# Another order of the same operations in a hand-planned attention and feed-forward kernel

The kernel runs on one core of one Trainium2 chip. The metric is the time of one execution on the device, in microseconds (us); lower is better. All runs named here gave correct results.

Names: PE is the tensor engine, PEld its weight loads, DVE is VectorE, ACT is ScalarE, POOL is GpSimd, SP is SyncE. An engine's name with a q behind it (SPq, POOLq) is its sequencer, which issues transfers.

## The reference

```python
# q, k, v: 8 batches x 8 heads x 576 rows x 64; w_phi: 64 x 128
def phi(x):
    proj = einsum('bhsd,df->bhsf', x, w_phi)
    proj = proj - max(abs(proj), axis=-1, keepdims=True)
    return concatenate([exp(proj), exp(-proj)], axis=-1)
q_p, k_p = phi(q), phi(k)
kv  = einsum('bhsf,bhsd->bhfd', k_p, v)
z   = sum(k_p, axis=2)
num = einsum('bhsf,bhfd->bhsd', q_p, kv)
den = einsum('bhsf,bhf->bhs', q_p, z)[..., None] + 1e-06
x   = (num / den) with heads joined            # 4608 tokens x 512
out = (maximum(x @ w_gate, 0) * (x @ w_val)) @ w_out    # 512 -> 1536 -> 512
```

Linear attention comes first, then a gated feed-forward layer on its output. The feed-forward matmuls are four fifths of PE's work. They can begin only when the first rows of `x` are there, so the kernel has a *head* (load, project, k'v, divide, transpose, with PE often waiting), a *middle* (feed-forward of one batch woven with the attention of later batches) and a *tail* (last copy, last stores).

## The kernel before

The kernel writes down every operation once, with what it depends on and which buffers and PSUM banks it needs. It then replays them in the order of a text table. An entry `34P00` is operation 34, on PE, with slots 0 and 0 for the buffers that it opens; the letters are P (PE), A (ACT), D (DVE), G (POOL) and S (SP). `w29` is 29 warm-up matmuls on a tile of zeros, `z3` are three of them in the next operation's own bank. The table is one global list, but each engine sees only its own entries, in that order.

```python
def read(self, table):
    order, last_load, last_turn, zeros = [], None, None, 0
    for entry in table.split():
        if entry[0] == "w":
            order += [(self.warm(), PE)] * int(entry[1:])
            continue
        ...
        n, letter, slots = re.fullmatch(r"(\d+)([A-Z])(\w*)", entry).groups()
        o, e = self.ops[int(n)], LETTERS[letter]
        new = [b for b in (*o.banks, *o.bufs) if b.slot is None]
        for b, slot in zip(new, slots, strict=True):
            b.slot = int(slot, 36)
        ...
        order.append((o, e))

# k_item: projection of k in two 64-row halves, then exp on ACT, maxima on DVE
for i in range(4):
    for x in range(2):
        half = slice(D * x, D * (x + 1))             # 64 rows
        nc.tensor.matmul(pair[x].t[:, F * i : F * (i + 1)],
                         lhsT=kT.t[half, 4 * u + i, :], rhs=w2[half, x, :])    # L390
...
# the scaling of V by the exponentials of the maxima, on POOL for the most part
eng.tensor_tensor(vs.t[:, :, :, 0:D], vn..., e()..., op=ALU.mult)              # L416
eng.tensor_copy(vs.t[:, :, :, D], e())                                         # L423

# q_cols: the same for q, again in 64-row halves
nc.tensor.matmul(pair[x].t, lhsT=w2[half, x, :], rhs=cols(half))               # L507

# k_kv (L483) and q_num (L601): 128-row matmuls of 65 columns
# q_num's end: xu = u * r on POOL (L629), then a transpose and a copy to xT
# ffn: four matmuls of 512 columns a group (L670 up, L708 down)

# the stores of the last group of rows: each tile of 128 rows goes to two batches
for x, e in enumerate((SP, ACT) if t == 3 else (SP, SP)):
    def store_part(x=x, e=e, t=t, place=place, lo=lo, hi=hi):
        r0 = S * (2 * t + x) + SF
        engines[e].dma_start(out=out[r0 : r0 + SM, lo:hi],
                             in_=place()[SM * x : SM * (x + 1), lo:hi])        # L735
    op(e, 0.5, store_part, [c_], [ob], ...)
```

## Time and profile before

| | the kernel before |
|---|---|
| time, median of the first three runs | 379.24 us (378.41 to 379.54) |
| profiled span | 377.3 us |
| first feed-forward matmul starts at | 31.4 us |
| warm-up matmuls | 146 |
| waits of PE (start to start, beyond the usual spacing) | 17.8 us |
| end of the last matmul to end of the span (*) | 4.8 us |

(*) Here and below a matmul is counted as done one spacing (0.22 us for 512 columns) after its start. The trace's modelled end of the last matmul lies 0.16 us later; the 4.6 us of the prediction are counted from there.

The rows of the page that carry the argument are quoted in the prediction. The difference between 379.24 and 377.3 is time outside the profiled instructions. This profile was taken in a run of 379.24 us.

### The profile page before, as it was taken

How to read it: one execution, taken by the hardware profiler on the slowest of the kernel's cores; microseconds unless marked ns; L12 is line 12 of the kernel's file. 1: busy time of each engine (PE TensorE's matmuls, PEld its weight loads, DVE VectorE, ACT ScalarE, POOL GpSimd, SP SyncE). 2: the span in 40 equal slices, each digit the busy share in tenths (PEclk: the TensorE clock that was granted, in tenths of full speed). 3: DMA queues.
4: the chain of work that ended last, by engine and by line, in shares of the span. 5: the costliest groups of instructions: out<-in, count | busy, mean ns of one | idle time of the engine just before them, and what ended most of it. 6: DMA issues, size and time to landing. Idle time of an engine off the chain costs nothing.

```text
span 377.3 us, 8560 instructions
## 1 busy us (share of the span) xinstructions
PE 365.1 (97%) x3259; PEld 206.3 (55%) x3305; DVE 264.4 (70%) x642; ACT 232.8 (62%) x532; POOL 172.0 (46%) x206
## 2 busy tenths in 40 slices
PE   8889999999999999999999999999999999999995
PEld 7677797445656555464455544654465544444452
DVE  5989998777897977868965887679748645234121
ACT  5989975699599557756894569669853121222211
POOL 8698773459594335592693237713641300000000
PEclk9999999999999999999999999999999999999999
DMA  8999976798967593899667244951200500011016
GB/s 152 245 214 238 198 107 105 136 267 149 153 137 112 110 228 85 144 153 181 136 141 159 84 86 114 166 120 30 70 2 15 127 2 27 14 48 65 0 57 167
DMA packets 83288, 44.73 MB, mean 119 GB/s; under 512 B 54064, under 2 KB 76464, under 8 KB 83248
## 3 DMA queue, kind: packets, MB, share of 16 engines
q0 software_dynamic: 32656, 23.27, 36.4%
q1 hardware_dynamic: 50352, 20.75, 24.8%
q8 instruction: 26, 0.43, 0.5%
q10 hardware_dynamic: 240, 0.16, 0.2%
q14 instruction: 14, 0.11, 0.1%
HBM read 37.81 MB, written 9.44 MB: 125 GB/s over the span
## 4 chain that ended last, share of the span: by engine, by line
PE 88%; POOL 4%; ACT 3%; DVE 2%; issue 1%; DMA 1%; SPq 0%; POOLq 0%; DVEq 0%
PE ps L670 49%; PE ps L708 24%; PE ps L601 5%; PE ps L483 4%; PE ps L507 2%; PE ps L390 2%; ACT kp L351 2%; POOL vs L416 1%; DMA w<-in_w_phi_dram 1%; DVE mq L517 1%; POOL xu L629 1%; PE ps L642 1%; PE ps L532 0%; POOL wg_sb L297 0%; PE ps L437 0%
## 5 line engine op out<-in xcount | busy, mean ns | idle before, releaser
L676 ACT CAST val<-ps 128x512 bf16<-128x512 f32 (+1 forms) x120 | 64.9, 569 | 76.6 <-PE ps L670 68.1
L679 DVE SCALAR_TENSOR_TENSOR h<-ps,val 128x512 bf16<-128x512 f32 (+1 forms) x120 | 73.4, 626 | 43.9 <-PE ps L670 28.1
L708 PE MATMUL ps<-wo_sb,h 128*128 128x512 bf16 (+1 forms) x422 | 100.4, 373 | 1.1
L670 PE MATMUL ps<-xT,wg_sb 128*128 128x512 bf16 (+1 forms) x418 | 95.7, 354 | 0.7
L670 PE MATMUL ps<-xT,wv_sb 128*128 128x512 bf16 (+1 forms) x423 | 95.7, 355 | 0.5
L351 ACT ACTIVATE qp<-ps 128x512 bf16<-128x512 f32 x144 | 80.4, 643 | 11.4 <-PE ps L507 10.2
L629 POOL TENSOR_TENSOR xu<-u,r 128x512 bf16<-128x512 f32 x36 | 37.3, 1042 | 105.7 <-DVE r L626 58.2
L351 ACT ACTIVATE kp<-ps 128x512 bf16<-128x512 f32 x128 | 71.4, 631 | 9.7 <-PE ps L390 8.1
L416 POOL TENSOR_TENSOR vs<-vn,ek 128x1024 bf16<-128x1024 f32 x31 | 59.1, 1906 | 23.2 <-ACT ek L364 14.9
L670 PEld LDWEIGHTS <-wv_sb 128*128 128x128 bf16 x480 | 44.0, 98 | 40.4 <-issue 1.9
L670 PEld LDWEIGHTS <-wg_sb 128*128 128x128 bf16 x480 | 44.5, 98 | 39.4 <-issue 0.7
L708 PEld LDWEIGHTS <-h 128*128 128x128 bf16 x444 | 41.1, 98 | 44.8 <-issue 1.6
L401 DVE TENSOR_REDUCE mk<-ps 128x4 f32<-128x512 f32 x64 | 41.4, 676 | 2.9 <-PE ps L390 1.5
L517 DVE TRANSPOSE_TENSOR_REDUCE mq<-ps 128x16 f32<-128x512 f32 x56 | 37.5, 695 | 6.1 <-PE ps L507 3.1
L616 DVE TENSOR_TENSOR u<-ps,t 128x195 f32<-128x195 f32 (+3 forms) x120 | 37.2, 329 | 2.0
L601 PEld LDWEIGHTS <-qp 128*128 128x128 bf16 x640 | 30.4, 98 | 14.2 <-issue 0.2
L609 DVE TENSOR_TENSOR t<-ps,cq 128x195 f32<-128x195 f32 (+1 forms) x84 | 26.2, 329 | 15.1 <-PE ps L601 12.6
L601 PE MATMUL ps<-kv,qp 128*128 128x65 bf16 x640 | 33.7, 193 | 0.1
L483 PEld LDWEIGHTS <-kp 128*128 128x128 bf16 x512 | 21.7, 98 | 6.0 <-issue 2.1
L483 PE MATMUL ps<-vs,kp 128*128 128x65 bf16 x512 | 23.1, 193 | 1.9 <-POOL vs L423 1.8
L483 PE MATMUL ps<-vsm,kpm 128*128 128x65 bf16 x128 | 20.6, 193 | 0.0
L719 DVE COPY ob<-ps 128x512 f32<-128x512 f32 x16 | 10.9, 679 | 10.2 <-PE ps L708 7.6
(95 smaller groups left out, 322.4 us busy)
## 6 DMA issues: line engine op xcount, KB each, us to landing
out_dram<-ob SPq DMA_DIRECT2D x32, 256.0 KB, 2.7
vn<-in_v_dram POOLq DMA_DIRECT2D x7, 1024.0 KB, 8.3
kn<-in_k_dram POOLq DMA_DIRECT2D x7, 512.0 KB, 8.5
qn<-in_q_dram POOLq DMA_DIRECT2D x7, 512.0 KB, 7.7
wo_sb<-in_moe_w_out_dram POOLq DMA_DIRECT2D x1, 1536.0 KB, 15.3
vn<-in_v_dram POOLq DMA_DIRECT2D x2, 512.0 KB, 9.2
vm<-in_v_dram POOLq DMA_DIRECT2D x16, 64.0 KB, 6.2
wv_sb<-in_moe_w_val_dram POOLq DMA_DIRECT2D x2, 512.0 KB, 13.5
```

The costliest lines, as they stand in the source:

```text
L351: nc.scalar.activation(dst(s), ps.t.rearrange("p (c f) -> p c f", f=f), AF.Exp, scale=sign)
L401: nc.vector.tensor_reduce(m.t.rearrange("p (i x) -> p x i", x=2)[:, x], ps.t.rearrange("p (c f) -> p c f", f=F), axis=AX.X, op=ALU.max, ap ...
L416: eng.tensor_tensor(vs.t[:, :, :, 0:D], vn.t[:, 2 * u : 2 * u + 2].rearrange("p h c d -> p (h c) d")[:, :, None, :] .to_broadcast([P, 2 * ...
L483: nc.tensor.matmul(acc[:, hh, s, :], lhsT=lhsT, rhs=rhs, start=(n == 0), stop=(n == 19))
L517: nc.vector.tensor_reduce(mdst(x), ps.t.rearrange("p (h j t) -> p h j t", j=NQ, t=32), axis=AX.X, op=ALU.max, apply_absolute_value=True, a ...
L601: nc.tensor.matmul(ps.t[:, E * (2 * i + s): E * (2 * i + s + 1)], lhsT=qp.t[:, s, h, :], rhs=kv_of[b][h // 2][0].t[:, h % 2, s, :],)
L616: nc.vector.tensor_tensor(u.t[rows, lo : lo + n], ab[:, :, 0], t.t[rows, 0:n], op=ALU.add)
L629: eng.tensor_tensor(xu.t, u.t[:, :, 0:D], r.t.to_broadcast([P, H, D]), op=ALU.mult)
L670: nc.tensor.matmul(ps.t[:, 0:n], lhsT=w[:, dc, P * fi : P * fi + P], rhs=xt()[:, dc, lo:hi], start=(dc == 0), stop=(dc == NDC - 1),)
L676: nc.scalar.copy(val.t[:, 0:n], pv.t[:, 0:n])
L679: nc.vector.scalar_tensor_tensor(h.t[:, fi, lo:hi], pg.t[:, 0:n], 0.0, val.t[:, 0:n], op0=ALU.max, op1=ALU.mult,)
L708: nc.tensor.matmul(ps.t[:, lo:hi], lhsT=h.t[:, fi, P * t : P * t + P], rhs=wo_sb[:, fi, lo:hi], start=(fi == 0), stop=(fi == NFC - 1),)
```

## The change

Only the order table differs. The change's own description: the order was searched again with eight loads in flight on Pool's queue, against the mean of the planned landing times and of ones some tenths of a us later, so that a plan does not hang on a load landing exactly on time. The 129 changed lines hold the same operations, with 61 letters changed (32 operations, copies and small exponentials, go from DVE to ACT, 29 of the same kinds the other way), 130 warm-ups instead of 146, and other slots. The first lines, the rest cut:

```diff
 ORDER = """
-0G 5D 10S 6D 9S 7G 11G0 2S 1S 8S 16G0 15G w29 34P00 12G0 32P1 4D 35A 3D 13G0 60P230000 33A 66A 61D
-w6 50P451111 14G 55A 64D 52A 54D 21G1 63A 51D 65A 17G w28 38P6 62A 36P0 40P10 39D 57A 22G0 53A 41D
...
+0G 6D 10S 9S 7G 11G0 2S 1S 8S 13G0 5D w29 34P00 12G0 32P1 4D 15G0 35A 3D 60P230000 16G 33D 65A 61D
+w9 50P451111 14G 66A 51D 55A 21G1 64D 56A 53A 54D w26 36P6 18G 67A 52A 38P0 40P10 37D 62A 39D w4
...
```

What it does to Pool's queue (11 is a half of k, 12 and 14 the halves of v, 13 the rest of v, 15 and 16 the halves of q, 21 and 22 the next batch's k, 17 to 20, 27 and 28 weight pieces, 25 the next q, 59, 69 and 79 the scalings of V):

```
before  11 16 15 12 13 14 21 17 22 25 19 20 27 59 18 69 79 ...
after   11 13 12 15 16 14 21 18 22 59 69 25 79 19 17 28 20 27 ...
```

## The prediction

> **What bounds the kernel now.** I read the header of the page first, then the busy time of each engine in stretches of 20 us, then the Pool engine's timeline of the first 20 us, then PE's waits.
>
> ```profile
> span 377.3 us, 8560 instructions
> PE 365.1 (97%) x3259; PEld 206.3 (55%) x3305; DVE 264.4 (70%) x642; ACT 232.8 (62%) x532; POOL 172.0 (46%) x206
> ```
>
> PE is busy for 97% of the span, but that figure hides waits, because matmuls overlap. So I took the start of each matmul in the trace and asked how far apart starts are when nothing holds them: 215.8 ns for 512 columns (a piece of 31 on the chain that ended last takes 6.69 us), 30.3 ns in the groups of 20 that make k'v, 31.7 ns in the groups that multiply by it, 56 ns for a 128x128 warm-up matmul. With those spacings the work is: feed-forward, 1296 matmuls of 512 columns or their equal, 279.9 us (864 in the two up projections 186.6, 432 in the down projection 93.2, rounded apart); 640 at 30.3 ns, 19.4 us; 640 at 31.7 ns, 20.3 us; the smaller groups (projections, transposes, maxima) 26.1 us. Sum 345.7 us, which no order can change. The rest of 377.3 is: 1.0 us before the first matmul, 146 warm-up matmuls x 56 ns = 8.2 us, waits 17.8 us (start-to-start time beyond the spacings), and 4.6 us from the end of the last matmul to the end of the last store. The time of a run, 379.24, is 1.9 us above the span.
>
> ```profile
> core 0: us, PE busy (x) PEld busy (x) DVE busy (x) ACT busy (x) POOL busy (x), PEclk, DMA share, GB/s
> 0.00:20.00 20.00, 16.45 (x224) 14.40 (x224) 15.79 (x35) 15.06 (x37) 15.39 (x26) 1.00 1.12 198
> 20.00:40.00 20.00, 18.52 (x297) 14.87 (x295) 18.52 (x54) 18.96 (x48) 17.23 (x20) 1.00 1.24 226
> 40.00:60.00 20.00, 20.00 (x273) 16.97 (x271) 18.17 (x53) 16.75 (x46) 14.32 (x18) 1.00 1.00 136
> ...
> 300.00:320.00 20.00, 19.89 (x120) 9.62 (x120) 9.93 (x23) 3.42 (x6) 0.00 (x0) 1.00 0.07 20
> ```
>
> By stretch, the 17.8 us of waits lie 7.2 in the first 20 us, 3.9 in the next 20, and only 6.8 in all the rest. The warm-ups are all in the first 31.4 us, before the first feed-forward matmul. So 11.1 + 8.2 = 19.3 us of what an order can win lies in the head. In 20 to 40 us VectorE and ScalarE are over 90% busy and the DMA share is at its cap: the head is bound by several engines at once, not by PE. After 40 us PE is the bound. In the head Pool is blocked in its own queue:
>
> ```profile
> 8.16 0.76 POOL L297 DMA_DIRECT2D wv_sb<-in_moe_w_val_dram  x1 [0.46 <-DMA kn<-in_k_dram]
> 9.91 0.62 POOL L270 DMA_DIRECT2D km<-in_k_dram  x1 [0.99 <-DMA qn<-in_q_dram]
> 11.31 0.61 POOL L270 DMA_DIRECT2D km<-in_k_dram  x1 [0.78 <-DMA qn<-in_q_dram]
> 13.02 0.89 POOL L256 DMA_DIRECT2D qn<-in_q_dram  x1 [1.10 <-DMA vn<-in_v_dram]
> 14.47 0.76 POOL L297 DMA_DIRECT2D wv_sb<-in_moe_w_val_dram  x1 [0.56 <-DMA vm<-in_v_dram]
> ...
> 16.74 1.92 POOL L416 TENSOR_TENSOR vs<-vn,ek 128x1024 bf16<-128x1024 f32 x1
> 18.90 0.28 PE L483 MATMUL ps<-vs,kp 128*128 128x65 bf16 x4 [1.34 <-POOL vs L423]
> ```
>
> The ninth load on the queue waits for the landing of the first, the tenth for the second, and so on: eight are in flight. The first scaling of V (16.74) stands behind these issues, and the first k'v group on PE waits for it.
>
> **What the Trainium skill says.** "Trainium Kernel Development and Optimization", Performance Expectations, calls matmul busy time a bad metric because matmuls are pipelined. The trace agrees: 97% busy hides 26 us of waits and warm-ups. "TensorE: Matmul & The Clock Gate", section "Wait — 56ns, not 53.3ns?", gives warm start-to-start times of 55.6 and 215.7 ns for 128 and 512 columns; I measure 56 and 215.8. "Trainium Kernel Development and Optimization", Key Constraints, says DMAs issued from all queues run on the same 16 engines and interleave. In the trace, loads from 5.7 to 49 us land one after another at intervals that follow their size (about 1.3 us for the 256 KB weight pieces, 7.6 us for the 1536 KB one), so a landing depends on what stands ahead in the queue.
>
> **The change part by part.** Nothing is computed differently; I compared the orders engine by engine.
>
> *Removed:* 16 of the 146 warm-ups, 16 x 56 ns = 0.9 us. They fill planned idle time, so this is worth at most 0.9 us and only if the work behind them is ready.
>
> *Moved, loads:* before, Pool issued k, two of q, then v. Now it issues k, the rest of v, v, then q. From the spacing of landings I expect the first half of v at about 11.2 us (12.74 before), and the halves of q at about 12.6 and 14.0 (9.63 and 11.02 before). Weights: the first gate piece now comes before the next batch's remaining k, the value pieces later, at an estimated 24 to 26 us. They are wanted at about 31.
>
> *Moved, V scaling on Pool:* before, one q load and three weight loads stood between the last blocked k load and the first scaling. Now the first two scalings come right after that k load. Their input on ScalarE is ready at an estimated 11.5 us (eight exponentials of about 0.5 us from 6.85, then two small ones). So the first scaling starts at about 11.6 instead of 16.74, and the last of Pool's three ends at about 20 instead of 23.6: 3.6 us earlier.
>
> *What of this reaches the end:* little. The first feed-forward matmul needs both first chunks of xT. I added up what VectorE must do, in its order, until the reciprocals of these chunks, at the start-to-start times of the trace (0.62 a maximum, 0.30 a t or u, 0.35 a copy): before 21.7 and 23.7 us of work, now 21.2 and 23.8. ScalarE until the xT copy: 25.5 before, 25.2 now. From 6.8 us to the first feed-forward matmul VectorE sat idle for about 1.5 us and ScalarE for 1.3. That idle time is all that earlier Pool work can give back. I take two thirds, 1.0 us, plus 0.3 us for ScalarE's shorter order: 1.3 us off the head. PE has 12.3 us of work ahead of the first feed-forward matmul in both orders.
>
> *Middle:* after 40 us PE has 6.8 us of waits, in many pieces under 0.3 us. Groups are shuffled everywhere, but VectorE and ScalarE work per stretch of PE work is as even as before. I give 0.3 us of gain.
>
> *Tail:* both orders end with the same last four-matmul group, one copy on ScalarE and two stores. The stores before it have over 1 us each. 0.0.
>
> Sum: -1.3 - 0.3 = -1.6 us; 379.24 - 1.6 = 377.6 us.
>
> **The rivals.** (1) The head gives back more, because Pool was the critical engine: the chain that ended last runs on Pool almost without a break from 16.74 to 34.5 us. If VectorE and ScalarE had only been waiting in its shadow, 3.6 us would come off, giving 375.6. Against it: Pool's first division waited 0.36 us for VectorE's reciprocal at 26.87, so VectorE was as late as Pool. (2) The bound moves to the loads: q lands 3 us later, and five weight loads are now issued after the scalings, so the DMA queue may run dry near 22 us. Then q's maxima come late and the first feed-forward matmul slips by 1 to 2 us: 380 to 381. For it: the DMA share is at its cap in the head. Against it: K work and V scaling can fill the time meanwhile, and weights have some 5 us to spare. (3) The shuffled middle meets other bank and buffer waits. It has 340 us in which to gain or lose; half more waits would be +3.4 us, 381; half fewer -3.4. A plan made on later landings should be more robust, not less.
>
> **Range and chances.** The head could go from -3.6 to +1.5 and the middle by 1.5 either way; together I expect 8 in 10 within -4.0 and +1.2 us: 375.2 to 380.4. Faster by 2% needs 7.6 us, which is 29% of all waits and warm-ups together; 2%. Slower by 2% needs waits in the middle to double; 2%. Within 2%: 96%.
>
> **What would show it right or wrong.** Right: Pool's first V scaling starts before 13 us and no load issue blocks it; the first k'v group no longer waits for Pool; the first feed-forward matmul starts between 29.5 and 31 us (31.4 before); PE's waits after 40 us stay between 5 and 8 us; the time from last matmul to end stays near 4.6 us. Wrong: a wait for q or for a weight piece ahead of the first feed-forward group, a feed-forward start after 31.4, or waits after 40 us that change by over 2 us either way.

## The result, and the profile after

The changed kernel took 378.84 us (median of 6 runs, 378.32 to 378.94); the kernel before took 378.64 us in the 6 runs beside it (378.41 to 379.54). The ratio is 0.9997, with a 95% interval of 0.9984 to 1.001: the same. Ratios here are the mean time of one kernel's runs over that of the other's runs of the same rounds, so they are not quite the ratio of the medians quoted. Executions over 1.5% slower than the fastest of the same kernel are left out of the means. All outputs are right.

The first line of the page of the changed kernel, and its busy times:

```profile
span 376.5 us, 8527 instructions
PE 364.2 (97%) x3242; PEld 205.7 (55%) x3289; DVE 263.0 (70%) x639; ACT 234.3 (62%) x535; POOL 172.7 (46%) x206
```

The span is 0.8 us shorter than that of the first profile of before, with PE as busy as ever. The stretches of the changed kernel that answer to those in the prediction (columns: stretch in us, its length, then busy time and number of instructions of each engine, granted clock, share of the DMA engines, GB/s):

```profile
0.00:20.00 20.00, 16.99 (x252) 14.77 (x253) 16.36 (x36) 15.02 (x37) 16.94 (x27) 1.00 1.13 200
20.00:40.00 20.00, 18.52 (x272) 14.88 (x269) 19.71 (x56) 20.00 (x53) 17.36 (x22) 1.00 1.18 209
```

VectorE is now busy for 19.7 of the 20 us from 20 to 40, and ScalarE for all of them, against 18.5 and 19.0 before. Pool's timeline in the changed kernel (columns: start, duration, engine, line, operation, output and input, count; in brackets the idle time ahead and what ended it):

```profile
7.81 0.76 POOL L297 DMA_DIRECT2D wg_sb<-in_moe_w_gate_dram  x1
8.55 1.25 POOL L270 DMA_DIRECT2D km<-in_k_dram  x2
11.00 1.91 POOL L416 TENSOR_TENSOR vs<-vn,ek 128x1024 bf16<-128x1024 f32 x1 [1.20 <-ACT ek L364]
...
16.98 1.90 POOL L416 TENSOR_TENSOR vs<-vn,ek 128x1024 bf16<-128x1024 f32 x1 [1.04 <-ACT ek L364]
```

No issue of a load stands blocked any more, and the first scaling of V starts at 11.00 instead of 16.74 us. It waits for ScalarE now, not for the queue. (The limit of eight is in the program: in the packed traces Pool's loads use eight completion semaphores, 108 to 115, in turn, and each blocked issue waits for the one that it is about to use again. No run here shows a limit of the chip.) On PE the first k'v group starts at 16.74 us without a wait; before it started at 18.90 after 1.34 us. The longest wait of PE in the head behind the first projection is for ScalarE now, and the first feed-forward matmul comes at 29.59 us (31.41 before, the first line here):

```profile
31.41 1.83 PE L670 MATMUL ps<-xT,wv_sb 128*128 128x256 bf16 x14
```

```profile
25.57 0.38 PE L322 MATMUL ps<-ident,kn 128*128 128x128 bf16 x4 [1.18 <-ACT qp L351]
...
29.59 0.60 PE L670 MATMUL ps<-xT,wv_sb 128*128 128x256 bf16 x4
```

The chain of waits by engine (page, part 4), of the kernel before and then of the changed one, shows the same thing from the end backwards: Pool has left it, and VectorE has grown. (The chain varies between executions: in the second profiles of both kernels Pool has 5% before and 1% after.)

```profile
PE 88%; POOL 4%; ACT 3%; DVE 2%; issue 1%; DMA 1%; SPq 0%; POOLq 0%; DVEq 0%
```

```profile
PE 87%; DVE 6%; ACT 4%; issue 1%; DMA 1%; SPq 0%; DVEq 0%
```

So the head did what it should, by 1.8 us against the first profile of before, and yet the median time rose by 0.2 us. Where did it go? To see that, I set both traces against the same ruler: the useful PE work done so far (345.7 us in all, no warm-ups). *Lost time* is time on the clock minus useful work done at that point.

| useful work done | lost, before (first profile) | lost, before (second) | lost, after (first) | lost, after (second) |
|---|---|---|---|---|
| 14 us, just into the feed-forward | 19.58 | 19.11 | 17.38 | 17.36 |
| 60 us | 21.59 | 21.12 | 19.99 | 19.98 |
| 345.6 us, the last matmul | 26.99 | 26.49 | 25.91 | 25.90 |

(The second profiles are those of the first two experiments.) The two profiles of the changed kernel agree within 0.02 us all the way. Those of the kernel before differ by 0.5 us, which arises in its first 20 us and stays constant after. Against the second one, the changed kernel leads by 1.7 us at 14 us of work, by 1.1 at 60, by 0.6 at the last matmul. The rest goes in the tail, in the sequencer that issues the last stores. Here are SP's issues in the kernel before and in the changed one:

```profile
369.43 2.52 SPq L735 DMA_DIRECT2D out_dram<-vn  x4
372.05 0.54 SPq L727 DMA_DIRECT2D out_dram<-ob  x1
372.64 1.76 SPq L735 DMA_DIRECT2D out_dram<-vn  x3
```

```profile
368.81 1.80 SPq L735 DMA_DIRECT2D out_dram<-vn  x3
370.65 0.59 SPq L727 DMA_DIRECT2D out_dram<-ob  x1
371.28 2.40 SPq L735 DMA_DIRECT2D out_dram<-vn  x4
```

One issue takes some 0.5 to 0.7 us, and they stand back to back. The last copy on ScalarE ended at 373.26 us before and at 372.18 us after. The last store was issued 0.55 us after that copy before (373.81), and 0.91 us after it in the changed kernel (373.09), because the issue begun at 371.85, of a store that had been ready before, held SP until 372.40. From the end of the last matmul to the end of the span it is 4.78 and 4.77 us in the two profiles of before, 5.14 and 5.07 in those of the changed kernel.

The account against the second profile of before, then: first feed-forward matmul 30.94 to 29.59 us, -1.35; from there to the end of the last matmul 341.04 to 341.81 us, +0.77; tail +0.37. Sum -0.21, the difference of the spans (376.76 and 376.54 us). Against the first profile the head's term is -1.82, the other two are +0.75 and +0.36, and the sum is -0.7.

### The profile page after: what moved, and what is told of

Read it like the earlier page. It is cut to its first block, busy times and chain, and to the rows that moved or that the text cites. A ratio compares the mean times of both kernels' runs of the same rounds, so it can differ in the third digit from the quotient of the medians.

```text
span 376.5 us, 8527 instructions
## 1 busy us (share of the span) xinstructions
PE 364.2 (97%) x3242; PEld 205.7 (55%) x3289; DVE 263.0 (70%) x639; ACT 234.3 (62%) x535; POOL 172.7 (46%) x206
## 4 chain that ended last, share of the span: by engine, by line
PE 87%; DVE 6%; ACT 4%; issue 1%; DMA 1%; SPq 0%; DVEq 0%
PE ps L670 48%; PE ps L708 23%; PE ps L483 5%; PE ps L601 5%; PE ps L507 2%; ACT kp L351 2%; PE ps L390 2%; DVE t L609 2%; DVE u L616 1%; DMA w<-in_w_phi_dram 1%; DVE h L679 1%; DVE mq L517 1%; PE ps L532 0%; PE ps L642 0%; PE ps L437 0%
## 5 line engine op out<-in xcount | busy, mean ns | idle before, releaser
L676 ACT CAST val<-ps 128x512 bf16<-128x512 f32 (+1 forms) x120 | 67.0, 587 | 74.2 <-PE ps L670 69.0
L351 ACT ACTIVATE qp<-ps 128x512 bf16<-128x512 f32 x144 | 82.3, 654 | 4.9 <-PE ps L507 3.6
L351 ACT ACTIVATE kp<-ps 128x512 bf16<-128x512 f32 x128 | 73.3, 660 | 11.8 <-PE ps L390 10.7
L601 PE MATMUL ps<-kv,qp 128*128 128x65 bf16 x640 | 34.9, 194 | 0.1
L719 ACT COPY ob<-ps 128x512 f32<-128x512 f32 x18 | 10.9, 608 | 16.8 <-PE ps L708 16.8
```

The lines of the kernel that those rows point to most:

```text
L351: nc.scalar.activation(dst(s), ps.t.rearrange("p (c f) -> p c f", f=f), AF.Exp, scale=sign)
L601: nc.tensor.matmul(ps.t[:, E * (2 * i + s): E * (2 * i + s + 1)], lhsT=qp.t[:, s, h, :], rhs=kv_of[b][h // 2][0].t[:, h % 2, s, :],)
L676: nc.scalar.copy(val.t[:, 0:n], pv.t[:, 0:n])
```

## The experiments

Twelve kernels ran. The runs of the kernel before have the medians 379.26, 378.93 and 379.0 us, 11 runs each. The expectations call some theories by a letter, and count the end as the table above does. In short: A says that the head really gained and that the new order gives part of it back later; P says that the order of Pool's queue alone makes the head's gain; Q says that Pool's order and those of the other engines fit only each other; S is about the price of changing between 64-row and 128-row matmuls; T is about the stores at the end; H is about the first load of `w_phi`; N says that the removed warm-ups were worth nothing.

**1. The kernel before once more.** No edit.

> The kernel before, unchanged, run again as a kernel of its own, to see how much two profiles and two sets of runs of one program differ. If the profile of before that I predicted from was typical, its first feed-forward matmul starts at 31.4 us again and its span is 377.3 us. If that profile was a slow execution (its run took 379.2 us, the median of six is 378.64), the span is some 0.6 us shorter and the 0.6 us shows in the head or in the waits of the middle. Ratio to before 1.000 in either case.

Measured: 378.72 us (378.55 to 379.44), 0.9989 (0.9973 to 1.0006) of the same kernel's runs beside it; so 0.1% is noise here. The profiled span is 376.8 us, 0.5 less than in the first profile. The clock went to full speed at 5.80 us (5.11 in the first profile), PE's first k'v group waited less for Pool, and the first feed-forward matmul came at 30.94 us. Pool's first scaling, then PE's lines:

```profile
16.26 1.95 POOL L416 TENSOR_TENSOR vs<-vn,ek 128x1024 bf16<-128x1024 f32 x1
```

```profile
30.94 0.61 PE L670 MATMUL ps<-xT,wv_sb 128*128 128x256 bf16 x4
```

```profile
18.45 0.28 PE L483 MATMUL ps<-vs,kp 128*128 128x65 bf16 x4 [0.15 <-POOL vs L423]
```

The issues of loads stand blocked in this profile too, by up to 1.13 us. What follows: the 1.34 us wait that the prediction leaned on was a trait of one execution. Half a microsecond of what looked like the change's gain is the spread of the kernel before; which of its two profiles is nearer to the typical run, their times (379.24 and 378.70, about a median of 378.97) don't say.

**2. The changed kernel once more.** No edit.

> The changed kernel, unchanged, run again. Theory A (the head's gain of 1.8 us is real, and 0.7 us of it is given back by waits after 45 us, the rest lost in executions with a granted clock of 0.996 to 0.998): first feed-forward matmul at 29.6 us again, span 376.5 us with clock 1.0 and 377.0 us otherwise. Theory B (the head's gain was a lucky execution): first feed-forward matmul between 29.6 and 31.4 us. Ratio to before 0.9997 within 0.001 in either case.

Measured: 378.56 us (378.03 to 380.02), 0.9986 (0.9966 to 1.0007); span 376.5 us. The replay is steady: once its loads have landed, these two executions run to 0.02 us alike. So differences between two orders that arise after the first 20 us can mostly be trusted to about a tenth, though the runs' times can't tell them apart. It is no guarantee: in the profile of experiment 12 one wait, at the k'v group near 117 us, is 0.44 us longer. The head itself varies: with this same head the first feed-forward matmul starts at 29.57 to 30.13 us in seven profiles of this page.

**3 and 4. The head of one order on the rest of the other.** To see whether head and rest can be told apart, I joined the tables after 345 operations and gave some buffers (six and eight) other slots at the seam.

```diff
 # after_head
-(the changed order from operation 346 on)
+(the order of before from operation 346 on)
 # before_head
-(the order of before from operation 346 on)
+(the changed order from operation 346 on)
```

> The changed order for the first 345 scheduled operations (some 45 us), the order of before from there on; buffers reassigned where the two did not fit (6 of them). Theory A: it keeps the head's gain of 1.8 us and does not give back the 0.7 us in the middle, so about 1.8 us faster than before at the last matmul, 376.9 us, ratio 0.995. Rival C (what the head wins is lost later whatever the order, since PE then runs against the same loads and evictions): ratio 0.9995 to 1.000.

> The order of before for the first 345 scheduled operations, the changed order from there on (8 buffers reassigned). Theory A: no gain in the head and the changed middle's loss of 0.7 us, so 379.3 us, ratio 1.002. Rival C: the middle is as good as the other, ratio 1.000.

Measured: `after_head` 378.96 us (378.47 to 379.57), 0.9993 (0.9977 to 1.0009); `before_head` 380.85 us (380.51 to 381.07), 1.004 (1.0025 to 1.0055). The seam spoils both as tests of the whole time. PE stands there for a value that the joined order makes too late. First `after_head`, then `before_head`:

```profile
50.16 0.30 PE L601 MATMUL ps<-kv,qp 128*128 128x65 bf16 x4 [0.59 <-DVE kv L490]
...
52.54 0.60 PE L670 MATMUL ps<-xT,wv_sb 128*128 128x256 bf16 x4 [0.34 <-ACT qp L351]
```

```profile
50.82 0.60 PE L670 MATMUL ps<-xT,wv_sb 128*128 128x256 bf16 x4 [0.56 <-ACT cq L547]
```

In `after_head` the seam costs some 1.2 us or more, most of what the head gained. Past the seam the traces can be read. From 35 us of useful work to the last matmul, the lost time grows by 6.0 us in the kernel before (20.98 to 26.99) and by 6.3 in `after_head`, which runs that order; by 6.6 in the changed kernel (19.29 to 25.91) and by 6.6 in `before_head`, which runs that one. So the rest of the changed order is 0.3 to 0.6 us worse than that of before, whatever head it has. That is theory A in the middle; its size is small.

**5. Pool's new order alone.** The table of before, with only the G entries in the changed kernel's order (and moved as early or late in the list as that needs); every other engine's list is untouched.

```diff
-0G 5D 10S 6D 9S 7G 11G0 2S 1S 8S 16G0 15G w29 34P00 12G0 32P1 4D 35A 3D 13G0 ...
+0G 7G 11G0 13G0 12G0 15G0 16G 14G 21G1 18G 22G0 5D 10S 6D 9S 2S 1S 8S w29 34P00 32P1 4D 35A 3D ...
```

> The kernel before with Pool's queue alone in the changed order up to its last division for the first batch (loads of v ahead of q, the three scalings of V ahead of the blocked loads); PE, VectorE, ScalarE and SP exactly as before. Theory P (the head's gain is Pool's queue, which stood blocked behind eight loads in flight): first feed-forward matmul 1.3 us earlier than in the second profile of before, at about 29.6 us. Theory V (VectorE and ScalarE bind the head, and their own order makes the gain): under 0.5 us earlier, 30.5 us or more. Theory Q (q lands later and the old order of PE wants it early): first feed-forward matmul later than 31.0 us.

Measured: 381.2 us (380.59 to 382.71), 1.0061 (1.004 to 1.0082). The first feed-forward matmul starts at 31.77 us, 0.8 later than in the second profile of before and 0.4 later than in the first. PE transposes q early in this order, and q now lands late; Pool is free early and then waits for ScalarE:

```profile
12.87 0.62 PE L322 MATMUL ps<-ident,qn 128*128 128x128 bf16 x8 [1.89 <-DMA qn<-in_q_dram]
```

```profile
12.62 1.90 POOL L416 TENSOR_TENSOR vs<-vn,ek 128x1024 bf16<-128x1024 f32 x1 [2.25 <-ACT ek L364]
...
20.36 1.90 POOL L416 TENSOR_TENSOR vs<-vn,ek 128x1024 bf16<-128x1024 f32 x1 [2.80 <-ACT ek L364]
```

Pool's queue alone gains nothing: theory P falls.

**6. Everything but Pool's new order.** The changed table with the G entries in the order of before.

```diff
-0G 6D 10S 9S 7G 11G0 2S 1S 8S 13G0 5D w29 34P00 12G0 32P1 4D 15G0 35A 3D 60P230000 16G ...
+0G 7G 11G0 16G0 15G 12G0 13G0 14G 21G1 17G 22G0 25G1 19G 20G 27G 6D 10S 9S 2S 1S 8S 5D w29 34P00 ...
```

> The changed kernel with Pool's queue alone put back to the order of before in the head; the other engines in the changed order. Theory P: first feed-forward matmul back at 31.0 us or later, time 1.3 us up, ratio to before about 1.002. Theory V: it stays near 29.6 to 30.2 us, ratio 0.999 to 1.000. Theory Q: the other engines of the changed order want v early and q late, so it is worse than either kernel, at 32 us or later.

Measured: 381.16 us (380.79 to 382.39), 1.0059 (1.004 to 1.0078). The first feed-forward matmul starts at 33.47 us, 3.9 us later than in the changed kernel, and the delay stays to the end. But this profile fell on the slowest of the six runs (382.39 us), so some 1.2 us of it may be that execution's. PE, which now asks for k'v early, stands for Pool:

```profile
19.54 0.28 PE L483 MATMUL ps<-vs,kp 128*128 128x65 bf16 x4 [2.14 <-POOL vs L423]
22.34 0.28 PE L483 MATMUL ps<-vs,kp 128*128 128x65 bf16 x4 [0.89 <-POOL vs L423]
```

Each half of the change, put alone on the kernel before, makes the runs 0.6% slower (2.3 us), and each of these twelve runs is slower than the median of either kernel; together they bring the first feed-forward matmul 1.35 us forward. Theory Q holds: the gain belongs to no part, but to orders that agree on what is wanted first.

**7. More changes between 64-row and 128-row matmuls.** In the middle, PE changes 60 times between the projections, which use 64 rows of the array (L390, L507), and the 128-row matmuls. This holds for both orders. In the traces the start-to-start time at such a change is longer than the spacing by a median of 96 ns in each direction. At changes from one operation to another within 128 rows, some 260 after 44 us, the median is under 1 ns. To test that this is the price of the change and not a chance wait, I moved 10 feed-forward groups (not fourteen, as the expectation says) to stand between two neighbouring 64-row groups each, so that PE changes 20 times more.

```diff
-382G 404P640403 1483A 414P372025 425D 1488P0 407A ...
+382G 1488P0 404P640403 1483A 414P372025 425D 407A ...
 (and 9 more such moves)
```

> The changed kernel with fourteen feed-forward groups of PE moved one or two places ahead, between two groups of 64-row matmuls that stood together: 104 instead of 84 changes between 64-row and 128-row matmuls after 50 us or so by my count of PE's order; VectorE, ScalarE, Pool and SP exactly as in the changed kernel. Theory S (each such change costs PE a fixed 96 ns, so most of PE's lost time after 45 us is this): 20 x 0.096 = 1.9 us more lost at the last matmul, ratio to before about 1.004. Rival W (that lost time is waits for buffers and evictions, which this does not touch): 0.3 us or less.

Measured: 383.86 us (383.37 to 384.13), 1.012 (1.0103 to 1.0138). After 44 us the trace has 80 changes, again with a median of 96 ns each. Together they now take 8.3 us against 5.8, with the waits that fall on them. The time rose by far more than 20 x 96 ns = 1.9 us, since groups moved off their places wait for banks and inputs that are not ready, for example:

```profile
78.39 1.46 PE L670 MATMUL ps<-xT,wg_sb 128*128 128x512 bf16 x6 [0.58 <-ACT kp L351]
```

The price of one change stands, by its median. The size of this experiment was underrated, and it shows how little slack the order has.

**8. One store earlier in SP's list.** Of the two stores of the same tile, one stood far back in the changed order.

```diff
-... 2017D0 2022P 2019S 1946P ... 2029D 1943S 2031A 2004P 2018S 2030S
+... 2017D0 2022P 2019S 2018S 1946P ... 2029D 1943S 2031A 2004P 2030S
```

> The changed kernel with one store of SP's queue (the second half of the third last-group tile, ready 5 us before the end) issued next to its first half instead of among the last four. Theory T (the last stores stand in line on SP, four issues of 0.6 us each in a row, and this is the 0.3 us that the end grew by): time from the last matmul to the end of the span 4.7 us again instead of 5.0, all else as in the changed kernel, ratio 0.999 against it. Rival: the end is set by the landing of the last store alone and stays at 5.0 us.

Measured: 378.16 us (377.96 to 381.64), 0.999 (0.9958 to 1.0022). From the last matmul to the end it is 5.06 us, as in the changed kernel. SP still issues without a pause:

```profile
367.09 1.70 SPq L727 DMA_DIRECT2D out_dram<-ob  x1
...
369.37 1.76 SPq L735 DMA_DIRECT2D out_dram<-vn  x3
371.17 0.58 SPq L727 DMA_DIRECT2D out_dram<-ob  x1
371.85 1.74 SPq L735 DMA_DIRECT2D out_dram<-vn  x3
```

The end did not come earlier in this profile. The first line says why: the next store after the moved one held SP for 1.70 us, against 0.57 in the changed kernel:

```profile
366.44 0.57 SPq L727 DMA_DIRECT2D out_dram<-ob  x1
```

So the place that was gained was lost again before the end. What made this issue long, and whether it is long in every execution, one profile can't say. The times don't refute theory T: five of the six runs took 377.96 to 378.42 us, as fast as those of experiment 9. It stays open here; the next experiment tests it in another way.

**9. Two queues for the last stores.** The changed kernel, with one of the two stores of three of the last tiles on ScalarE's queue instead of one tile only.

```diff
-for x, e in enumerate((SP, ACT) if t == 3 else (SP, SP)):
+for x, e in enumerate((SP, ACT) if t != 2 else (SP, SP)):
```

> The changed kernel with the second-half stores of the first and second tile of the last group issued on ScalarE's queue instead of SP's; nothing else. The end in the changed kernel: the last two stores are issued 0.3 and 0.9 us after the last copy ends, because SP has a row of issues of 0.59 us each. Theory T2 (the end is SP's issue time): last issue within 0.3 us of the copy's end, time from the last matmul to the end of the span 4.3 us instead of 5.1, ratio against the changed kernel 0.998. Rival: the landing of stores or ScalarE's own issue sets it, 4.8 us or more.

Measured: 378.02 us (377.62 to 378.39) beside 379.0 (378.47 to 379.89) of before, 0.9975 (0.9963 to 0.9986). This is the lowest median (experiment 8 has 378.16), and the only interval that lies below 1. It is against the kernel before, so it holds the reordering's part too. Against the changed kernel no runs stand side by side; that kernel with its 16 warm-ups back took 378.64. Both last stores are issued at 372.50 us, 0.03 us after the last copy. SP's list, then ScalarE's:

```profile
371.13 1.84 SPq L735 DMA_DIRECT2D out_dram<-vn  x3
```

```profile
371.88 0.58 ACT L719 COPY vn<-ps 128x512 f32<-128x512 f32 x1 [2.88 <-PE ps L708]
372.50 0.50 ACTq L735 DMA_DIRECT2D out_dram<-vn  x1
```

From the last matmul to the end it is 4.59 us instead of 5.07 to 5.14. I had expected 4.3: the store on ScalarE's queue took 2.61 us to land (at 375.11) and became the last. Not all of the gain shows in the span (376.3), since this execution happened to lose 0.28 us more in its first 12 us than those of the changed kernel's profiles.

**10. The best of all parts.** Two queues, the store moved, and three places where neighbouring blocks of 64-row groups were joined, to save changes.

```diff
-for x, e in enumerate((SP, ACT) if t == 3 else (SP, SP)):
+for x, e in enumerate((SP, ACT) if t != 2 else (SP, SP)):
 (and 64-row groups of three places joined into longer runs)
```

> The two queues for the last stores, and three pairs of blocks of 64-row matmuls joined by moving the second block up: 78 instead of 84 changes between 64-row and 128-row matmuls (another bank rotation follows from it). Theory S: 6 x 0.096 = 0.6 us less lost in the middle, so with the end's 0.8 us about 1.4 us below the changed kernel: 377.3 us, ratio to before 0.996. Rival: the joined blocks make bursts for ScalarE and VectorE, and waits for banks eat the 0.6 us: ratio 0.998 to before.

Measured: 383.24 us (382.7 to 383.4), 1.0106 (1.0091 to 1.012). The joined projections fill banks faster than ScalarE empties them, and PE stands; just after, the records have the granted clock at half speed for 3.41 us from 85.33 us.

```profile
83.61 0.37 PE L507 MATMUL ps<-qT,w 64*128 64x512 bf16 x1 [1.25 <-ACT val L676]
84.60 1.19 PE L708 MATMUL ps<-wo_sb,h 128*128 128x512 bf16 x4 [0.62 <-ACT qp L351]
```

At this place alone 3.9 us are lost, some 1.7 of them by the slow clock (half of 3.41), against the few changes saved at 96 ns each. The rival that feared bursts was right, by more than it said.

**11. The same, with SP's load of half of `w_phi` ahead of its loads of k.**

```diff
-0G 6D 10S 9S 7G 11G0 2S 1S 8S 13G0 5D w29 ...
+0G 6D 2S 10S 9S 7G 11G0 1S 8S 13G0 5D w29 ...
```

> As the last one, with SP's load of half of w_phi issued ahead of its two loads of k instead of behind them. PE's longest single wait of the changed kernel is 1.2 to 1.5 us at 4.6 us for this weight, which lands at 5.5 us; issued 1.0 us earlier it should land near 4 us, and k's two loads 0.5 us later. Theory H (the head's engines start when w_phi is there and all of the head moves with it): first feed-forward matmul 0.5 us earlier. Rival (k's later landing takes its place): 0 to 0.3 us later.

Measured: 382.86 us (380.73 to 387.12), 1.0083 (1.0061 to 1.0105). PE's first projection waits less for `w_phi`, but the loads of k behind it come later and PE waits for those. The feed-forward starts at 29.46 us, 0.3 us earlier than in experiment 10, but the kernels with the changed head as it was start it anywhere from 29.57 to 30.13. The wait moved to k, and a gain of 0.1 to 0.7 us is all that the profile leaves for the theory. Its runs scatter with the clock: those with a granted clock of 1.0 took 380.73 and 381.41 us, three with a clock of 0.996 took 382.8 to 383.0.

**12. The 16 warm-ups put back.** The changed kernel with 16 more warm-ups at one place of the head.

```diff
-... 69G 85A w7 42P0 76A ...
+... 69G 85A w23 42P0 76A ...
```

> The changed kernel with the sixteen warm-up matmuls that it has fewer put back, at the place where PE waits 0.8 us for q at 13.2 us: 146 again. Theory N (warm-ups fill time in which PE would wait, taking them out gave nothing): first feed-forward matmul within 0.15 us of the changed kernel's 29.6 to 30.0 us, ratio to before unchanged near 0.999. Rival (they take PE time, 16 x 56 ns): 0.9 us later, ratio 1.001.

Measured: 378.64 us (378.28 to 380.57), 0.9997 (0.9978 to 1.0015): the changed kernel's time. The profile fell on its slowest run (380.57 us), in which the clock reached full speed only at 10.42 us. It had lost 1.94 us by 2 us of useful work, ahead of the added warm-ups, and 1.84 at every later point of the head; the added warm-ups themselves lie in a wait (until 14.08 us in the changed kernel, for ScalarE and not, as expected, for q) and cost nothing at this place. So taking them out gained nothing that shows: theory N holds.

## Why the prediction was right, and where it was not

The forecast of "within 2%" and the range held: 378.84 us lies between 375.2 and 380.4. That says little, for no change at all (379.24) would have lain there too. The middle value, 377.6, was 1.2 us too low: of the forecast gain of 1.6 us the spans show 0.2 to 0.7, and the runs' times none that is clear of noise. By its own steps:

**Warm-ups, "worth at most 0.9 us".** No worth of theirs shows (experiment 12).

**Loads and V scaling.** The first half of v was predicted at 11.2 us and landed at 9.89; the halves of q at 12.6 and 14.0, and landed at 11.06 and 12.37. The first scaling was predicted at 11.6 and started at 11.00; the last of the three ended at 18.9, earlier than the 20 predicted. The step was right, with every landing over a microsecond too late: the rest of v is small and moved ahead of the large pieces at less cost than the spacing of landings suggested.

**Head, -1.3 us.** Measured -1.35 against the second profile of before, and -1.82 against the first, from which the forecast was worked out. Over all profiles with an untouched head, three of before (30.79 to 31.41 us, mean 31.05) and seven of the changed kernel (29.57 to 30.13, mean 29.80), it is -1.25. So the size was right. The reason held as well: ScalarE's idle time came back. Here are the stretches from 6.80 us to the first feed-forward matmul, of the second profile of before and of the changed kernel (the third, fourth and fifth busy times are VectorE, ScalarE and Pool):

```profile
6.80:30.94 24.14, 22.07 (x390) 18.16 (x389) 23.02 (x58) 23.04 (x58) 20.29 (x25) 1.00 1.32 237
```

```profile
6.80:29.59 22.79, 20.60 (x366) 17.00 (x365) 22.28 (x58) 22.74 (x58) 19.53 (x23) 1.00 1.28 202
```

ScalarE stood idle for 24.14 - 23.04 = 1.10 us before and for 22.79 - 22.74 = 0.05 us after; its work became 0.30 us shorter. That is 1.05 + 0.30 = 1.35 us, against the 1.0 + 0.3 predicted. From the first profile (6.80 to 31.41 us: ScalarE busy for 23.25 of 24.61 us) it is 1.31 + 0.51 = 1.82. So the agreement of the two parts to the tenth is luck: the share was wrong, for ScalarE gave back nearly all of its idle time and not two thirds, and its shorter work counted for more in one reading. VectorE's idle time fell from 1.12 to 0.51 us (1.76 in the first profile, where the prediction says 1.5). So the first rival, Pool as the one critical engine with 3.6 us to gain, was wrong for the reason given, that VectorE and ScalarE were as late. (Its chain from 16.74 to 34.5 us is not almost all Pool: 2.2 us of it, from 30.1 to 32.3, lie on PE and VectorE.) What the prediction missed is that neither Pool's order nor the others' gives any of it alone (experiments 5 and 6). How much of the 1.35 us is due to which engine's order can't be said for that reason.

**Middle, -0.3 us: this step failed.** It cost +0.8 us. The prediction called the 6.8 us after 40 us "waits, in many pieces under 0.3 us", as if a better order could win any of them. After 44 us, 6.5 us of excess in the kernel before and 7.0 in the changed one contain 60 changes between 64-row and 128-row matmuls, at a median of 96 ns, 5.8 us. No order with the same blocks can win those, and both orders have the same number there. What is left for waits is about 1 us in either, which left little room for a gain of 0.3. Experiments 3 and 4 show that the loss belongs to the order of the rest. A count start by start of the traces shows where it lies. From the first feed-forward matmul on, the changed order has 68 changes between 64-row and 128-row matmuls and that of before 66, which is 0.2 us. After 44 us PE stands in five places of the changed order, in both its profiles: at 52.6 us (0.14), 113.2 (0.09), 116.6 (0.16), 226.1 to 226.5 (0.39) and 294.3 (0.06); in the order of before in two, again in both profiles: at 49.1 (0.12) and 224.6 (0.13), by the second one's times. What each of these waits for is not settled.

**Tail, 0.0: this step failed too.** It cost +0.37 us. "Both orders end with the same last four-matmul group, one copy on ScalarE and two stores" is true, but I did not count the issues that SP has still ahead of them. They take up to 0.7 us each, and one of them held SP when the last copy ended, which put off the last store by 0.36 us; with fewer stores on SP the end came 0.5 us earlier (experiment 9).

**The signs that were named.** Pool's first scaling before 13 us, no blocked issue, no wait of k'v for Pool, a feed-forward start between 29.5 and 31 us, and PE's waits after 40 us between 5 and 8 (7.4): all held. The time from the last matmul to the end "near 4.6 us" did not: 5.0 by the same count, from the trace's end of the last matmul.

**Rivals.** The second, that late loads would bind, shows only in experiment 5. The third, a shuffled middle, came true in sign and at under a quarter of its size.

## What to carry to other kernels

In a head where several engines are nearly full, add up each engine's idle time up to the point that matters. Here the gain was the idle time of the fullest engine and what the new order took off its own work; it was not the longest wait in the profile, and only the orders of all queues together gave it. Before calling gaps on PE waits, count what is fixed in them, such as the changes between 64-row and 128-row matmuls. And at the end, count the issues on each queue after the last data are ready: spreading them over two queues was one line and took 0.5 us (0.13%) off the end in the traces.

## What the Trainium skill lacked or had wrong

- "TensorEngine Tiling (Array Packing)", section Key Properties, says that changing the tiling mode drains the tensor engine, and gives no time for it. The traces show time lost at such changes: a median of 96 ns for each change between 64-row and 128-row matmuls, 60 of them in either order and 80 in experiment 7.
- "DMA: Bandwidth & Descriptors", section "Anatomy of one DMA — SWDGE (gpsimd) path", puts the sequencer's dispatch at about 50 ns and the fixed cost of a transfer at about 2 us, for transfers issued from GpSimd. For stores issued from SP, the time from issue to landing is near that (2.35 us, 373.09 to 375.44), but each of the last stores held the sequencer for 0.46 to 0.60 us, and in the changed kernel that put off the end by 0.36 us. For SP and ACT the page has a sequencer time of a plain copy only as a cycle count of earlier generations, in its comparison with trn3.
- "TensorE: Matmul & The Clock Gate", section "Part 1: The HAM clock gate (the "warmup" mystery)", calls the warm-up run-variable; the traces agree (full speed between 4.29 and 10.42 us). It gives the idle window that brings the slow clock back as about 3.4 us, and its section "A second HAM failure mode: psum-queue depth-cycling" says that short idles between groups can do it as well, without their lengths. In experiment 10 the clock fell to half for 3.41 us after waits of 1.25 and 0.62 us within 3 us, with a matmul between them.
